# Moving the raw pair of heads to the front of a hand-ordered attention and expert kernel

## The chip, the cores and the metric

The kernel runs on one core of a Trainium2 chip. The metric is the time of one execution on the device in microseconds (us); of several runs the median is given. The core has engines that run side by side, each through its own instructions in order: TensorE (PE in the profile, with PEld for its weight loads), VectorE (DVE), ScalarE (ACT), GpSimd (POOL) and SyncE (SP). POOL, SP and ACT also start transfers (DMAs), which 16 DMA engines carry out.

## The reference

Sliding-window causal attention (8 batches, 8 heads, 576 positions, head size 64, window 64), then an expert layer: each batch picks one of 8 experts by its pooled attention output, and runs all its rows through that expert.

```python
scores = scale * np.matmul(q, k.transpose(0, 1, 3, 2))
mask = (rel >= 0) & (rel < window)
scores = np.where(mask, scores, -1000000000.0)
attn = np.exp(scores)
attn = attn / (np.sum(attn, axis=-1, keepdims=True) + 1e-09)
attn_out = np.matmul(attn, v)
...
x = np.ascontiguousarray(attn_out.transpose(0, 2, 1, 3)).reshape(B, S, H * D)
pooled = x.mean(axis=1)
logits = pooled @ w_gate
e_idx = np.argmax(logits, axis=1)
...
h = np.maximum(x[mask] @ w1[e], 0.0)
out[mask] = gate_w[mask, None, None] * (h @ w2[e])
```

## The kernel before, in words

The work of a batch is cut into five units: four pairs of heads over the first 512 positions, and a fifth "tail" unit for the last 64 positions of all heads. Units are numbered through the batches: 0 to 3 are the pairs of batch 0 and 4 its tail, 5 to 8 and 9 belong to batch 1, and so on to 39. Pair 1 holds heads 2 and 3.

The order of all instructions is written out by hand in the list `OPS` (lines 2 to 38), which has 890 entries. A loop at line 537 runs through it and issues for each entry the instructions of one step. Each step belongs to one engine, and each engine executes its own steps in the order of the list. An entry has a letter, perhaps a small letter for the engine or the buffer, and a number: of the unit, of the batch, or of a transfer.

Steps of a unit, in the order in which they depend on each other:

- `T` (line 214): on PE, transposes of the pair's queries and keys into PSUM, 16 matmuls (8 for a tail). With `m` the result goes to one of three shared PSUM buffers (`mo`, in turn), without it to a buffer of its own, of which there is one.
- `U` (line 238) copies the transposed queries to SBUF, `k` (line 249) the keys; `a` stands for ACT and `d` for DVE.
- `S` (line 257): scores on PE. With `b` the mask is first added by two matmuls with the identity (line 269), without it the later step `K` (line 295) multiplies by the mask on DVE. With `m` the scores take two of the three shared PSUM buffers, else they go to one buffer pair of their own.
- `E` (line 279): exponential on ACT. One instruction, or two where the scores lie in two shared buffers.
- `l` (line 303): row sums on PE. `n` and `R` (lines 347 and 354): logarithm and exponential of its negative on ACT, which give the reciprocal of the sum.
- `A` (line 318): attention times V on PE. `X` (line 360): on DVE, times the reciprocal, with a running sum for the gate.

Steps of a batch: `g`, `j`, `G`, `H`, `I` compute the gate (lines 378 to 439), `P` (line 411) reads the number of the expert into a register of POOL, `V` (line 148) shifts V in SBUF by two copies on DVE, for which four of the batch's five V transfers must have landed. Expert steps: `c` issues the next chunk of expert matmuls on PE (a batch has nine for the first weight and nine for the second, lines 450 and 494), `ra` and `rd` empty a chunk's PSUM buffer on ACT or DVE, `O` and `o` store a result.

Transfers: `Q` (line 104) loads queries (even number) or keys (odd) of a batch for all heads, or for some of them (`Q0.48`: queries of batch 0, heads 4 to 7; `Q1.2`: keys of batch 0, heads 0 and 1; `Q3`: all keys of batch 1). `L` (line 137) loads a fifth of a batch's V (`L4`, `L9` and so on are half as large), `t` (line 130) the tail rows of queries and keys, `W` (line 416) a quarter of the picked expert's weights: `W0` and `W1` of the first weight of batch 0, `W2` and `W3` of the second. All of these are issued by POOL, and POOL's transfers, which convert from float32, share one software queue. Only `Y` (line 116) differs: it brings queries (`Y0.24`) and keys (`Y1.24`) of heads 2 and 3 of batch 0 over SP's queue, raw in float32, and `Cd` (line 123) converts them on DVE. This is the pair that comes raw, unit 1.

Setup: `i` makes the identity and `y` the band of the mask on POOL (lines 176 and 180), `mb` and `Mb` build the masks on DVE (lines 186 and 199), `z` clears parts of the V buffers on DVE (line 195).

The loads of queries, keys and tails have three buffers each, and V has three, so a transfer for batch 3 waits until batch 0's data have been read.

Of the kernel before, what the change touches and what calls it, by code (L numbers as in the profile page):

```python
# [1 line left out]
OPS = (  # L2
    "Y0.24 Q0.48 Q1.48 Q0.2 Cd0.24 y i Q1.2 Y1.24 Q3 Cd1.24 z Tm3 Tm2 mb T0 Tm1 ka3 ka2 ka0 "
    "t0 Ud3 Ud2 Q2 Sb3 L0 L3 ka1 L1 L2 E3 Smb2 L4 Ud0 l3 Ud1 t1 S0 T4 E2 kd4 Ud4 n3 Smb1 E0 "  # L4
    "Mb K0 E1 R3 Q4 L9 Tm5 Sb4 Tm7 Tm8 Ud5 Q5 ka5 kd8 E4 L5 kd7 l1 n1 T6 l4 n4 Ud7 l2 Sb5 ka6 "
    "n2 R1 R4 l0 V0 A3 Ud6 L7 Am1 n0 E5 T9 X3 Am2 Ud9 S7 R2 L8 E7 Ud8 X1 R0 l5 X2 L6 n5 Smb6 "
    "A0 Am4 K7 ka9 E6 t2 X4 X0 Sb8 l7 g0 n7 T12 j0 Q6 Sm9 Tm10 G0 Ud12 kd12 E8 Ud10 H0 E9 "
    "Tm13 Tm11 R7 K9 l6 R5 ka10 Sb12 Ud11 ka13 V1 n6 Q7 l8 P0 Ud13 W0 I0 kd11 T14 Am5 A7 X7 "
    "A6 Ud14 kd14 L12 n8 X5 E12 R6 l12 n12 Sm14 X6 S11 l9 E14 Smb10 Tm17 E11 n9 T18 W1 Ud17 "  # L9
    "A9 W2 E10 S13 kd18 Ud18 L13 Tm15 Ud15 l10 Am8 R8 W3 kd15 ka17 T16 K14 L11 c X8 L14 n10 "  # L10
    "E13 R9 c ra X9 c R10 c rd c g1 K11 rd S17 j1 G1 ra ra c H1 L10 c rd l14 K13 c t3 ra c P1 "
    "n14 Q8 ra c c rd c V2 Ua16 c c ra ka16 l11 A10 X10 Am12 W4 c Q9 R12 X12 n11 ra W5 R11 "
    "A11 rd W6 T19 E17 c l13 n13 R13 Ua19 I1 X11 c Sm18 S15 K17 L15 rd E18 W7 R14 A13 c l17 "
    "ra X13 A14 c L16 L17 X14 g2 n17 Tm20 E15 ra kd19 c Ud20 ra L18 kd20 T22 S19 Sm16 E19 L19 "
    "j2 G2 c P2 t4 K15 E16 Q10 K18 c ra c W8 H2 ra ka22 c ra c c S20 l18 ra rd rd K16 c n18 "
    "Q11 K19 L21 ra Tm21 c c Ua21 Ud22 l16 W9 T23 R17 kd21 L23 V3 c c R18 c ra Am17 Ud23 n16 "
    "ra l15 E20 X17 L22 c R16 ka23 c rd n15 A18 c S23 X18 Sm21 K20 T24 kd24 ra R15 E21 L20 "
    "A16 c l19 L29 ra L24 W10 n19 Ud24 Am15 X16 A19 W11 R19 c X15 l20 E23 n20 L25 I2 c X19 rd "
    "L26 ra Tm26 c g3 K23 kd26 l23 Ud26 R20 c ra Sm22 n23 S24 j3 rd G3 E24 E22 T28 H3 K21 c "
    "Tm27 Ud28 P3 t5 ka27 kd28 l21 L28 rd n21 I3 K24 S26 L27 T25 c V4 W12 c Ua27 ra l24 c K22 "  # L20
    "c ra ra ra Ud25 n24 c R23 Q13 Q12 Am20 X20 R21 c c c rd Am23 W13 kd25 E26 A21 T29 rd X23 "
    "l22 Sm27 W14 W15 n22 E27 S28 V5 c c K26 K27 L32 c R24 l26 c X21 t6 A24 E28 Am22 ra R22 "
    "L30 ra K28 n26 X24 Ud29 kd29 c A27 l27 n27 c X22 ra ra c g4 S25 R26 rd Sm29 j4 G4 L34 "
    "E29 T32 Tm30 kd30 E25 Ud30 c Ua32 H4 K29 P4 ka32 ra c l28 R27 T33 L33 rd Ua33 S30 I4 n28 "
    "c Q15 c ra L31 ra Am26 ka33 c E30 c ra W16 X27 X26 ra l29 c K25 R28 c rd n29 Q14 A28 K30 "
    "c W17 X28 T34 S32 Sm33 ra O O E32 c E33 c K32 l25 n25 R25 c kd34 Am25 A29 W18 c O Ua34 "
    "R29 rd W19 T31 l30 c X29 X25 rd ka31 g5 c c Ud31 O ra K33 rd Sm31 n30 S34 j5 G5 c V6 R30 "
    "P5 rd O E31 H5 c K31 T36 l32 Ud36 rd E34 c t7 c A30 c n32 I5 rd L39 ka36 ra R32 l33 T35 "
    "X30 A32 Ua35 L38 rd c K34 rd c ka35 c n33 T37 ra Sm35 S36 L37 O E35 rd c X32 ra E36 W20 "
    "l34 c L35 n34 c K35 K36 L36 c kd37 R33 c O l31 rd W21 R34 rd c n31 R31 c Ua37 Tm38 O W23 "  # L30
    "Ud38 A33 ra ka38 Am34 l35 T39 X33 c n35 W22 c ra X34 A31 X31 g6 kd39 c O Sm38 R35 O S37 "
    "ra E38 j6 c c G6 P6 Ud39 E37 ra ra c V7 K38 rd H6 c l36 c K37 W24 n36 S39 A35 l37 ra rd "
    "E39 c ra n37 c X35 R36 c A37 c ra l38 Am36 K39 ra c c O R37 rd X37 n38 Am39 X36 O c rd c "
# [560 lines left out]
```

## Time and profile before

| what | us |
|---|---|
| median of 3 runs (lowest to highest) | 204.35 (203.72 to 204.58) |
| the profiled execution's own time | 203.52 |
| its span in the trace | 201.9 |
| PE busy in the span | 183.5 |
| ACT busy | 131.8 |
| DVE busy | 119.9 |
| POOL busy (mostly issuing transfers) | 111.0 |

The profiled execution took 203.52 us, 1.6 more than the span that the trace covers. All rows of the trace count from the start of the span. A busy share is an average over a span whose parts have different limits, so it is read by stretches. In rows of the timeline the columns are start, duration, engine, line, operation, output and input, and in square brackets how long the engine had been idle and what ended that. In rows of groups the columns are busy us, mean ns of one, and idle time ahead with its releasers.

### The profile page before, as it was taken

What the parts mean: (1) busy time and instruction counts of PE and PEld (TensorE: products, weight loads), DVE (VectorE), ACT (ScalarE), POOL (GpSimd) and SP (SyncE); (2) the same over time, 40 slices, a digit from 0 to 9 for tenths busy, and PEclk for the clock granted to TensorE, in tenths of its full rate; (3) what the DMA queues carried; (4) which work ended last, traced back from release to release, by engine and by line L of the source; (5) the groups of instructions that cost most, each with busy time, mean ns of one, the idle gap of its engine ahead of it and who ended that gap; (6) DMA issues with size and microseconds to landing.
All of it is one profiled execution on the core that took longest, in us unless ns stands there. A gap on an engine that the chain in (4) does not pass through costs nothing.

```text
span 201.9 us, 8105 instructions
## 1 busy us (share of the span) xinstructions
PE 183.5 (91%) x3518; PEld 124.2 (62%) x3522; DVE 119.9 (59%) x347; ACT 131.8 (65%) x247; POOL 111.0 (55%) x158
## 2 busy tenths in 40 slices
PE   0487886899999999999999999999999999999991
PEld 0455564656677756577667666676656666776760
DVE  3527989595477546895877457966494651216410
ACT  2179998876599578977779975757787436321121
POOL 7985939235931593478633552439452716553561
PEclk9999999999999999999999999999999999999998
DMA  6999999999999999999999999999999999999693
GB/s 135 175 188 159 194 162 198 199 198 174 196 201 197 170 198 193 174 201 167 200 206 200 169 195 223 259 208 137 183 237 243 266 254 212 274 212 301 235 325 134
DMA packets 83346, 41.16 MB, mean 204 GB/s; under 512 B 48080, under 2 KB 80976, under 8 KB 83312
## 3 DMA queue, kind: packets, MB, share of 16 engines
q0 software_dynamic: 81936, 39.72, 138.5%
q1 hardware_dynamic: 768, 0.85, 1.3%
q8 instruction: 27, 0.44, 0.8%
q10 hardware_dynamic: 608, 0.08, 0.2%
q14 instruction: 7, 0.06, 0.1%
HBM read 61.88 MB, written 9.44 MB: 353 GB/s over the span
## 4 chain that ended last, share of the span: by engine, by line
PE 77%; DMA 9%; POOL 7%; issue 3%; DVE 2%; ACT 1%; POOLq 0%; DVEq 0%; ACTq 0%
PE ph L461 28%; PE po L503 25%; DMA vw<-in_v_dram 9%; PE tp L225 5%; PE ph L470 4%; PE s L275 4%; PE av L331 3%; PE po L512 3%; PE lb L309 3%; POOL vw L141 2%; POOL km L110 2%; POOL qm L110 1%; POOL out_dram L492 1%; PE gps L392 1%; POOL qkt L133 1%
## 5 line engine op out<-in xcount | busy, mean ns | idle before, releaser
L503 PE MATMUL po<-w2b,hm 128*64 128x512 f16 x512 | 60.1, 379 | 0.0
L461 PE MATMUL ph<-xm,w1b 128*64 128x512 f16 x512 | 60.0, 379 | 0.0
L461 PEld LDWEIGHTS <-w1b 128*64 128x64 f16 x512 | 31.7, 110 | 18.7 <-issue 0.4
L503 PEld LDWEIGHTS <-hm 128*64 128x64 f16 x512 | 30.1, 110 | 19.3
L141 POOL DMA_DIRECT2D vw<-in_v_dram x32 | 28.9, 910 | 13.3 <-DMA w1b<-in_moe_w_dram 4.3
L446 ACT ACTIVATE hm<-ph,gw 128x512 f16<-128x512 f32 x39 | 26.6, 693 | 13.4 <-PE ph L461 13.3
L492 POOL DMA_DIRECT2D out_dram<-ob x31 | 17.2, 557 | 25.0 <-DMA w1b<-in_moe_w_dram 7.0
L351 ACT ACTIVATE ln<-lb 128x512 f32<-128x512 f32 (+1 forms) x40 | 22.5, 563 | 11.8 <-PE lb L309 8.6
L364 DVE CUSTOM_DVE_ANT_0 xm<-av,rl 128x512 f16<-128x512 f32 x32 | 21.6, 686 | 10.4 <-PE av L331 9.5
L482 ACT COPY ob<-po 128x512 f32<-128x512 f32 x18 | 10.6, 586 | 23.6 <-PE po L503 23.6
L448 DVE TENSOR_SCALAR hm<-ph,gw 128x512 f16<-128x512 f32 x25 | 18.7, 748 | 12.1 <-PE ph L461 11.6
L357 ACT ACTIVATE rl<-ln 128x512 f32<-128x512 f32 (+1 forms) x40 | 23.3, 594 | 1.5 <-DVE pool L364 1.3
L225 PE MATMUL tp<-ident,qm 128*64 128x128 bf16 x256 | 13.8, 232 | 7.4 <-DMA qm<-in_q_dram 6.9
L288 ACT ACTIVATE pe<-s 128x1024 f16<-128x1024 f32 x19 | 19.5, 1028 | 1.4 <-PE s L275 0.7
L297 DVE TENSOR_TENSOR pe<-pe,mask 128x1024 f16<-128x1024 f16 x24 | 16.3, 687 | 3.9 <-ACT pe L288 3.1
L252 ACT COPY kT<-tp 128x512 bf16<-128x512 bf16 x19 | 11.2, 597 | 9.0 <-PE tp L225 8.0
L225 PEld LDWEIGHTS <-qm 128*64 128x64 bf16 x256 | 10.7, 118 | 10.0 <-DMA qm<-in_q_dram 6.9
L482 DVE COPY ob<-po 128x512 f32<-128x512 f32 x14 | 9.7, 690 | 10.7 <-PE po L503 10.5
L423 POOL DMA_DIRECT2D w1b<-in_moe_w_dram x16 | 12.6, 785 | 5.9 <-DMA vw<-in_v_dram 2.9
L275 PEld LDWEIGHTS <-kT 64*128 64x128 bf16 x576 | 10.1, 95 | 8.9 <-issue 5.6
L331 PEld LDWEIGHTS <-vw 128*64 128x64 f16 x512 | 12.4, 112 | 4.7 <-issue 1.2
L225 PE MATMUL tp<-ident,km 128*64 128x128 bf16 x256 | 13.9, 231 | 1.4 <-DMA km<-in_k_dram 0.9
(80 smaller groups left out, 267.2 us busy)
## 6 DMA issues: line engine op xcount, KB each, us to landing
w1b<-in_moe_w_dram POOLq DMA_DIRECT2D x16, 512.0 KB, 9.3
w2b<-in_moe_w_dram POOLq DMA_DIRECT2D x16, 512.0 KB, 13.4
out_dram<-ob POOLq DMA_DIRECT2D x31, 256.0 KB, 8.1
vw<-in_v_dram POOLq DMA_DIRECT2D x32, 128.0 KB, 9.0
km<-in_k_dram POOLq DMA_DIRECT2D x7, 512.0 KB, 9.3
qm<-in_q_dram POOLq DMA_DIRECT2D x7, 512.0 KB, 9.0
out_dram<-obt POOLq DMA_DIRECT2D x14, 64.0 KB, 7.7
qkt<-in_q_dram POOLq DMA_DIRECT2D x8, 64.0 KB, 7.6
```

Of the source, the lines that this page charges most:

```text
L141: nc.gpsimd.dma_start(out=vt[:, 2 * J + 1], in_=v[b, :, 128 * J:128 * J + 128].rearrange("h c d -> c h d"))
L225: nc.tensor.transpose(tp[p0:p0 + 64, n, r], t[:, 2 * i + hh, ts(r, 64)], ident)
L288: nc.scalar.activation(out=po, in_=sp[0], func=AF.Exp, scale=scale)
L351: nc.scalar.activation(out=ln, in_=lb[:, 0:n], func=AF.Ln)
L357: nc.scalar.activation(out=rl, in_=lns.pop((b, i)), func=AF.Exp, scale=-1.0)
L364: nc.vector.tensor_tensor_reduce(out=xm[:, i], in0=av.rearrange("q r p -> q (r p)"), in1=rl, scale=1.0, scalar=0.0, op0=ALU.mult, op1=ALU.add,
L446: nc.scalar.activation(out=o, in_=i, func=AF.Relu, scale=g)
L448: nc.vector.tensor_scalar(out=o, in0=i, scalar1=g, scalar2=0.0, op0=ALU.mult, op1=ALU.max)
L461: nc.tensor.matmul(out=ph[64 * c:64 * c + 64], lhsT=w1t[:, kb, ts(2 * ft + c, 64)], rhs=xm[:, kb], start=(kb == 0), stop=(kb == 3), skip_g ...
L482: copy(e)(out=ob, in_=po)
L492: (nc.scalar if n and eng is nc.sync else eng).dma_start(out=dst, in_=src)
L503: nc.tensor.matmul(out=po[64 * c:64 * c + 64], lhsT=hm[:, fb, ts(2 * r + c, 64)], rhs=w2t[:, fb], start=(fb == 0), stop=(fb == 7), skip_gr ...
```

## The change

The list `OPS` alone changes. Its first 262 entries are put in another order; the remaining 628 are the same. The number of units, chunks and transfers is the same, and so is the number of scores steps with `b` in the changed part (nine). Some steps change their engine or their buffer: in the changed part the k copies of units 0, 1, 3, 10 and 17 go from ACT to DVE and those of 7, 14 and 18 from DVE to ACT; the q copies of units 4, 7, 13 and 18 go from DVE to ACT and that of 16 from ACT to DVE; the scores of units 0, 7 and 14 gain `b`, those of 2, 5 and 8 lose it (and get a step `K` instead); several steps gain or lose `m`.

The raw pair's transposes, `T1`, stand first on PE, followed by `Tm3`, `Sb1`, `Tm2`, `T4`, `Smb3`, `Tm0`. On POOL the identity `i` moves ahead of the second load, the tails `t0` and the keys `Q3` of batch 1 ahead of the loads `Q0.2` and `Q1.2` of heads 0 and 1; later `L4` comes ahead of `L2`, `Q5` ahead of `Q4`, `t2` ahead of `L7`, `W1` to `W3` ahead of the V of batch 2, `Q8` ahead of `P1` and `t3`, and `L15` ahead of `W5`. The list up to where the two orders meet:

```diff
-    "Y0.24 Q0.48 Q1.48 Q0.2 Cd0.24 y i Q1.2 Y1.24 Q3 Cd1.24 z Tm3 Tm2 mb T0 Tm1 ka3 ka2 ka0 "
-    "t0 Ud3 Ud2 Q2 Sb3 L0 L3 ka1 L1 L2 E3 Smb2 L4 Ud0 l3 Ud1 t1 S0 T4 E2 kd4 Ud4 n3 Smb1 E0 "
-    "Mb K0 E1 R3 Q4 L9 Tm5 Sb4 Tm7 Tm8 Ud5 Q5 ka5 kd8 E4 L5 kd7 l1 n1 T6 l4 n4 Ud7 l2 Sb5 ka6 "
-    "n2 R1 R4 l0 V0 A3 Ud6 L7 Am1 n0 E5 T9 X3 Am2 Ud9 S7 R2 L8 E7 Ud8 X1 R0 l5 X2 L6 n5 Smb6 "
-    "A0 Am4 K7 ka9 E6 t2 X4 X0 Sb8 l7 g0 n7 T12 j0 Q6 Sm9 Tm10 G0 Ud12 kd12 E8 Ud10 H0 E9 "
-    "Tm13 Tm11 R7 K9 l6 R5 ka10 Sb12 Ud11 ka13 V1 n6 Q7 l8 P0 Ud13 W0 I0 kd11 T14 Am5 A7 X7 "
-    "A6 Ud14 kd14 L12 n8 X5 E12 R6 l12 n12 Sm14 X6 S11 l9 E14 Smb10 Tm17 E11 n9 T18 W1 Ud17 "
-    "A9 W2 E10 S13 kd18 Ud18 L13 Tm15 Ud15 l10 Am8 R8 W3 kd15 ka17 T16 K14 L11 c X8 L14 n10 "
-    "E13 R9 c ra X9 c R10 c rd c g1 K11 rd S17 j1 G1 ra ra c H1 L10 c rd l14 K13 c t3 ra c P1 "
-    "n14 Q8 ra c c rd c V2 Ua16 c c ra ka16 l11 A10 X10 Am12 W4 c Q9 R12 X12 n11 ra W5 R11 "
-    "A11 rd W6 T19 E17 c l13 n13 R13 Ua19 I1 X11 c Sm18 S15 K17 L15 rd E18 W7 R14 A13 c l17 "
+    "Y0.24 Q0.48 Y1.24 i Q1.48 y z Cd0.24 t0 Cd1.24 mb T1 Ud1 Tm3 Q3 kd1 Sb1 Tm2 Ud3 Q0.2 E1 "
+    "Q1.2 kd3 ka2 Ud2 T4 Smb3 L3 E3 Tm0 kd4 S2 Ud0 l1 Q2 kd0 E2 n1 Ua4 L0 Smb0 E0 Tm7 Ua7 T5 "
+    "R1 Tm8 L1 l3 Mb Sb4 Ud8 ka7 E4 n3 Ud5 Tm6 l4 L4 ka5 ka6 K2 Sb7 L2 n4 l2 kd8 t1 T9 V0 R3 "
+    "n2 Ud6 ka9 Sm5 A1 X1 R4 E5 Am3 X3 R2 Q5 Am2 K5 X2 l0 Smb6 A0 Ud9 L9 Q4 n0 l5 E7 n5 R0 "
+    "Am4 S9 t2 l7 E9 S8 n7 X4 L7 X0 L8 T12 E6 L5 g0 K9 j0 L6 Ud12 Tm10 Tm11 E8 G0 kd12 H0 T14 "
+    "Q6 R5 kd10 Ud14 l9 Ud11 Tm13 Ud10 kd11 I0 Sb12 Q7 n9 R7 l6 ka13 P0 W0 ka14 Smb14 V1 n6 "
+    "Ua13 W1 R9 Am5 W2 W3 E14 K8 Am6 E12 A7 X5 l8 R6 Smb10 L12 X7 X6 S11 n8 E11 l12 n12 T17 "
+    "kd17 S13 E10 A9 Tm18 X9 L11 ka18 Ud17 Tm15 Ua18 A8 K11 l10 L14 R8 kd15 Ud15 L10 T16 ka16 "
+    "c X8 E13 c L13 c n10 rd ra c ra g1 S17 j1 G1 R10 c rd c K13 c rd R12 ra c c H1 l14 rd c "
+    "ra Q8 n14 P1 c c l13 ra V2 c t3 Ud16 n13 W4 c ra A12 Q9 X12 E17 L15 l11 ra Am10 n11 c I1 "
+    "X10 R11 A11 W5 T19 rd c c K17 R13 X11 Sm18 Ua19 W6 S15 rd E18 W7 R14 A13 c l17 ra X13 "
...
```

34 rows, old and new, of the table OPS are left out of this document.

## The prediction

> **What bounds the kernel now.** I first read the stretches: the span cut where the chain of waits changes hands (columns: stretch, its length, then busy us and instruction count of PE, PEld, DVE, ACT, POOL, then clock, DMA share, GB/s).
>
> ```profile
> core 0 of [0], span 201.9 us
> ...
> 0.00:6.88 6.88, 0.00 (x2) 0.01 (x2) 3.33 (x14) 1.28 (x1) 5.49 (x13) 1.00 0.82 145
> 6.88:12.50 5.62, 4.37 (x65) 3.48 (x66) 1.68 (x5) 2.34 (x4) 5.32 (x7) 1.00 1.53 179
> 12.50:20.34 7.84, 6.54 (x158) 4.37 (x158) 3.99 (x10) 6.99 (x13) 5.01 (x7) 1.00 2.04 172
> 20.34:31.32 10.98, 8.87 (x235) 6.08 (x236) 9.53 (x34) 10.71 (x23) 7.65 (x10) 1.00 1.87 180
> 31.32:36.16 4.84, 2.88 (x102) 2.39 (x102) 4.78 (x12) 3.89 (x8) 4.48 (x6) 1.00 1.42 200
> 36.16:40.84 4.68, 4.18 (x126) 3.23 (x127) 2.31 (x7) 4.06 (x9) 1.45 (x2) 1.00 1.46 198
> ...
> 53.98:197.60 143.62, 143.53 (x2646) 97.12 (x2642) 86.04 (x242) 94.16 (x177) 73.29 (x106) 1.00 1.37 216
> ```
>
> From 53.98 on PE idles 0.09 us in 143.62: there the kernel is bound by PE, and that part of the list is unchanged. All idle time of PE that can be won lies ahead of the first expert chunk: 6.88 + 1.25 + 1.30 + 2.11 + 1.96 + 0.50 = 14.0 us. From 20.34 to 31.32 ACT is busy 10.71 of 10.98. Next I read the chain that ended last.
>
> ```profile
> 22.68 8.52 DMA vw<-in_v_dram
> ...
> 40.09 0.22 PE lb L309 x2
> 40.31 0.25 PE av L331 x16
> 40.56 0.45 PE tp L225 x16
> ...
> 45.33 0.34 PE s L275 x16
> ```
>
> Columns: start, length, what. It goes through a transfer of V, then stays on PE almost to the end. So PE is held at the start by loads, then by ACT and DVE, and the first chunk ("c1") is the point after which nothing is held. The change can move the end only by moving c1. The PE rows also give my prices on PE: row sums (l) 0.22, AV (A) 0.25, transposes of a pair (T) 0.45, scores (S) 0.34.
>
> Last the timeline, at the places that the order is about.
>
> ```profile
> 4.79 0.43 DVE L128 CAST km<-raw 128x512 bf16<-128x512 f32 x1 [0.35 <-DMA raw<-in_k_dram]
> ...
> 6.88 0.64 PE L225 MATMUL tp<-ident,qm 128*64 128x128 bf16 x8 [6.88 <-DMA qm<-in_q_dram]
> ...
> 8.83 0.64 PE L225 MATMUL tp<-ident,qm 128*64 128x128 bf16 x8
> ...
> 9.26 0.64 PE L225 MATMUL tp<-ident,km 128*64 128x128 bf16 x8
> ...
> 12.97 1.02 ACT L288 ACTIVATE pe<-s 128x1024 f16<-128x1024 f32 x1 [0.73 <-PE s L275]
> ```
>
> The raw pair is cast by 4.79 + 0.43 = 5.22, but PE stands at 6.88 for heads 6 and 7, and the first exponential runs at 12.97. Early transposes come 9.26 - 8.83 = 0.43 per eight, 0.86 a pair: half the later pace.
>
> **The change part by part.**
>
> *The loads are one line of transfers.* The tile view, over windows that hold one or two issues, gives times from issue to landing:
>
> ```profile
> L110 POOL DMA_DIRECT2D km<-in_k_dram x1: 790/790/790, 2.3 to 2.3; - x1
> DMA to landing us min/median/max: 6.0/6.0/6.0
> ```
>
> ```profile
> L110 POOL DMA_DIRECT2D km<-in_k_dram x2: 730/821/912, 4.8 to 5.5; - x2
> DMA to landing us min/median/max: 4.9/5.9/6.8
> ```
>
> ```profile
> L133 POOL DMA_DIRECT2D qkt<-in_k_dram x1: 688/688/688, 7.1 to 7.1; - x1
> DMA to landing us min/median/max: 6.1/6.3/6.5
> ```
>
> ```profile
> L110 POOL DMA_DIRECT2D km<-in_k_dram x1: 878/878/878, 27.8 to 27.8; - x1
> DMA to landing us min/median/max: 9.0/9.0/9.0
> ```
>
> ```profile
> L423 POOL DMA_DIRECT2D w1b<-in_moe_w_dram x1: 752/752/752, 30.0 to 30.0; - x1
> DMA to landing us min/median/max: 9.4/9.4/9.4
> ```
>
> Landings: Q1.48 at 2.3 + 6.0 = 8.3, Q1.2 at 9.7, Q3 at 5.5 + 6.8 = 12.3, the tails t0 at 7.1 + 6.1 = 13.2, Q7 at 36.8, W0 at 39.4. Q3 follows Q1.2 by 2.6 us and W0 follows Q7 by 2.6 us, both 512 KB: the transfers land in the order of their issue at about 200 GB/s. So a landing is set by what stands ahead of it on POOL's queue. Ahead of W0 stands the same set in both lists, so W0 stays at 39.4 whatever the engines do.
>
> *The head.* SP's two raw loads stay the first two of its queue. On POOL, `i` moves ahead of Q1.48 and `y` behind it (0.3 us later for Q1.48, hidden since the line is full), t0 ahead of Q3, and Q0.2 and Q1.2 behind both. `z` moves into DVE's wait for the raw rows: nothing. T1 then runs from about 4.5 to 5.9 instead of last. But T3 stands between it and Sb1, and its keys still land at 8.3 and take 0.43. Sb1 has no row at the slow pace: E1 starts between 8.75 + 0.34 = 9.1 and some 10.4 (an estimate: its 18 products at twice S's and T's later times), 2.6 us or more ahead of 12.97. I take 10.4; the next wait hides the difference.
>
> *The added wait.* Q1.2 now lands at 8.3 + 0.9 (t0) + 2.6 (Q3) + 0.65 + 0.65 (the halves of two heads, 2.6 / 4 each) = 13.1. PE stands at Tm0 until then. Queued behind it are S2, l1, Smb0, T7, T5, T8; Ud0 and kd0 on DVE and E2 and E0 on ACT wait for those. T 0.45, S 0.34: E2 starts about 14.0; an exponential takes 1.0 (the row at 12.97), n1 and Ua4 stand between, so E0 ends near 16.7. Before, four exponentials and n3 followed 12.97: near 17.4. The lead of 2.6 us has become 0.7.
>
> *Copies.*
>
> ```profile
> L252 ACT COPY kT<-tp 128x512 bf16<-128x512 bf16 x19 | 11.2, 597 | 9.0 <-PE tp L225 8.0 <-DVE qt L242 0.9
> ...
> L242 DVE COPY qt<-tp 128x512 bf16<-128x512 bf16 x25 | 10.4, 417 | 8.0 <-PE tp L225 3.6 <-ACT kT L252 3.2 <-PE s L275 1.2
> ...
> L252 DVE COPY kT<-tp 128x512 bf16<-128x512 bf16 x13 | 8.8, 684 | 2.8 <-PE tp L225 1.9 <-ACT qt L242 0.9
> ```
>
> ```profile
> 20.34 0.89 DVE L150 COPY vw<-vw 64x2048 f16<-64x2048 f16 x1 [0.54 <-DMA vw<-in_v_dram]
> ...
> 25.12 0.62 ACT L357 ACTIVATE rl<-ln 128x512 f32<-128x512 f32 x1
> ...
> 28.73 0.13 DVE L407 TENSOR_SCALAR gnm<-gmx 128x1 f32<-128x1 f32 x1
> ...
> 31.32 0.87 DVE L150 COPY vw<-vw 64x2048 f16<-64x2048 f16 x1
> ```
>
> Three k copies leave ACT's first stretch (3 x 0.60 = 1.8 us; 0.68 each on DVE, which waits at Tm0 anyway), but ka7, ka9, Ua4, Ua7 and n5 come ahead of R0, some 2.4 us with the tails (4, 9) at half price. So R0 starts near 25.12 + 0.6 = 25.7. V0 needs L2, which now has half a V transfer (L4, some 0.45) more ahead of it: 20.8 instead of 20.34, and A1, X1 and all behind them with it. V0 to gate is the same work on DVE less Ud8 (0.42), plus K9: the gate stays near 28.7, W0's issue near 30. DVE then has kd12, kd10, kd11, Ud11, Ud10 and the tail Ud14 ahead of V1, 3 x 0.68 + 2.5 x 0.42 = 3.1 us: V1 starts near 32.0 instead of 31.32, though its V rows land at 22.7 + 8.5 = 31.2 plus the 0.5 of t2, which moves ahead of L7. Up to here nothing is won.
>
> *The last stage before c1.* Here the gain arises.
>
> ```profile
> 38.68 0.38 PE L225 MATMUL tp<-ident,km 128*64 128x128 bf16 x7 [0.50 <-issue]
> ...
> 40.84 0.38 PE L461 MATMUL ph<-xm,w1b 128*64 128x512 f16 x2
> ```
>
> Before, PE is busy 4.18 of the 4.68 us up to c1 (the row 36.16:40.84): it is late with work, not with data, W0 having landed 1.4 us earlier. In the new order T14 and Smb14 come ahead of V1, and S10 ahead of T17. After Q7 lands at 36.8 PE has left: half of T17 0.22, S13 0.34, A9 0.13, T18 and T15 0.90, A8 0.25, l10 0.22, T16 0.45, together 2.5 us: 39.3. ACT's line: from R0 at 25.7 to the end of E10, which l10 needs, are 25 instructions; at the 10.98 / 23 = 0.48 us of the stretch in which it was full that is 37.7, and l10 comes at 38.7, so 1.0 us of waiting is covered. So PE is free for c1 at 39.3, and W0 lands at 39.4. I add 0.3 us for hand-overs between engines that such a sum leaves out (bounds: 0, and 0.73, V1's lateness in full) and take c1 = 39.75, a gain of 40.84 - 39.75 = **1.1 us**. The floor of W0 caps it at 1.4.
>
> *After c1* the steps up to A12 hold 14 chunks, as did those up to A10, and V2 caps the gain once more:
>
> ```profile
> 51.76 0.76 DVE L151 COPY vw<-vw 64x2048 f16<-64x2048 f16 x1
> ```
>
> ```profile
> 53.98 0.67 PE L331 MATMUL av<-pe,vw 128*64 128x64 f16 x32
> ```
>
> V2 ends at 52.5, and A10 began at 53.98: the same set of transfers stands ahead, so at most 1.4 can be kept; 1.1 passes. W1 to W3 move ahead of batch 2's V, L15 ahead of W5 and Q8 ahead of P1 and t3; I cost these at nothing. Their cover is PE's unbroken work from 53.98 on; without it W5, one V transfer of 0.9 us later, could hold PE by up to that. The list's last 628 entries are unchanged and carry the shift to the end.
>
> Sum against the profiled execution: 203.52 - 1.1 = 202.4; against the median 204.35, which is 0.8 above it: **203.2 us**.
>
> *A rule that speaks against it.* PE's transposes came 0.43 per eight at 8.83 and 0.45 per sixteen at 40.56. The Trainium skill, "TensorE: Matmul & The Clock Gate", section "Part 1: The HAM clock gate", says that an idle PE runs at half clock until a window of about 3.4 us was busy, and falls back after an idle one; the two rows agree, and the page would make nothing of the order itself but of its gaps. What follows from rows alone is rival C.
>
> **The rivals.** A: *DVE eats the gain.* V1 starts 0.7 us later than before, and PE's idle 0.50 at 38.68, whose cause the trace doesn't show, comes again. For: both lie on the path. Against: S14 and T14 are done by then. c1 = 39.35 + 0.73 + 0.50 = 40.6, a gain of 0.2: 204.1.
>
> B: *Slower, through Tm0.* If Q1.2 takes as long from its issue (about 7.1) as Q7 took, 9.0, instead of the 6.0 that my line of transfers comes to, it lands at 16.1, 3.0 later, and PE, ACT and DVE all stand. ACT, nearly full until 31.32, hands this on whole. From 1.1 us of lateness on the kernel is slower than before; at 3.0 c1 = 39.75 + 3.0 = 42.75, 1.9 worse: 206.3. For: nothing in the old order put whole loads ahead of these halves. Against: the line adds up so evenly.
>
> C: *PE stays slow.* Before, the slow pace lasted from 6.88 to about 12.5. The new order has gaps at 6 to 8.4 and at 13, so if the pace changes only after T0, T7, T5 and T8 cost 0.43 more each, 1.3 us, of which the wait for V0 hides some 0.5: c1 at 40.55, 204.1.
>
> **How the numbers follow.** Forecast 0.52, A 0.22, C 0.08, B 0.18. Forecast's own range: gain 0.7 to 1.4, 202.95 to 203.65, widened by the spread of a median. A measurement tells about 0.5%, 1.0 us, from no change. Of the forecast 0.42 lies beyond it. Faster 0.42; same 0.10 + 0.22 + 0.08 = 0.40; slower 0.18. The range reaches from the cap of 1.4 with half a us for the median's spread to a B of 1.9 us, and leaves out what lies beyond: 202.5 to 205.1.
>
> **What would show it.** Right: T1 before 5; PE idle at Tm0 until about 13; V0 near 20.8; V1 near 32; W0's landing at 39.4 and c1 within 0.5 behind it; later stages shifted alike. Wrong: W0 landing elsewhere (then the line of transfers is not a line), E10 after 39 (A), Tm0 after 14.5 (B), pairs still spaced 0.43 per eight after 14 (C), or PE idle between c1 and 60.

## The result and the profile after

The new order is slower: 205.28 us in the median of 22 runs (203.92 to 206.86) against 203.88 of 22 runs before (203.15 to 205.05), ratio 1.0069, 95% interval 1.0049 to 1.0089. I had forecast 203.2, with 0.18 on slower. The profiled execution took 206.8 us (span 205.2, before 203.52 and 201.9), so it lies at the long end of the new order's runs; the sums below are made against that execution, and the spread is taken up in the experiments. Ratios, here and below, leave out the few runs that lie over 1.5% above the fastest of their kernel.

First the stretches of the new kernel, cut where those of before were cut (stretch, its length, busy us and count of PE, PEld, DVE, ACT, POOL, then clock, DMA share, GB/s).

```profile
0.00:6.88 6.88, 1.91 (x24) 1.19 (x24) 4.01 (x18) 1.28 (x1) 5.46 (x13) 1.00 0.86 151
6.88:12.50 5.62, 4.50 (x54) 2.40 (x56) 2.22 (x5) 1.58 (x2) 5.17 (x7) 1.00 1.43 155
12.50:20.34 7.84, 3.89 (x93) 2.65 (x94) 1.45 (x4) 3.98 (x8) 3.83 (x5) 0.97 1.86 159
20.34:31.32 10.98, 9.15 (x208) 6.27 (x205) 7.84 (x24) 9.57 (x20) 7.64 (x9) 0.87 1.90 176
...
53.98:201.00 147.02, 146.81 (x2678) 98.83 (x2674) 87.54 (x245) 94.94 (x180) 76.17 (x110) 1.00 1.38 213
```

PE starts earlier, as it was meant to (1.91 us busy by 6.88, before 0.00). The head start is gone by 20.34: between 12.50 and 20.34 PE works 3.89 us instead of 6.54, DVE 1.45 instead of 3.99, ACT 3.98 instead of 6.99. All three stand, so they stand for something that none of them makes. The transfers too run at 155 and 159 GB/s where they ran at 179 and 172. The clock column shows 0.97, and in the next stretch 0.87. From 53.98 on PE is as full as before, so the loss must lie ahead of the first expert chunk (c1). PE's timeline at the place:

```profile
4.50 0.32 PE L225 MATMUL tp<-ident,qm 128*64 128x128 bf16 x2 [4.50 <-DVE qm L128]
...
13.24 0.41 PE L225 MATMUL tp<-ident,qm 128*64 128x128 bf16 x8 [0.16 <-DMA qm<-in_q_dram]
13.92 0.41 PE L225 MATMUL tp<-ident,km 128*64 128x128 bf16 x8 [0.27 <-DMA km<-in_k_dram]
...
15.48 0.41 PE L275 MATMUL s<-qt,kT 64*128 64x64 bf16 x16
19.42 0.41 PE L225 MATMUL tp<-ident,qm 128*64 128x128 bf16 x8 [3.52 <-DMA qm<-in_q_dram]
19.66 0.51 PE L225 MATMUL tp<-ident,km 128*64 128x128 bf16 x8
19.96 0.64 PE L225 MATMUL tp<-ident,qm 128*64 128x128 bf16 x8
20.38 0.64 PE L225 MATMUL tp<-ident,km 128*64 128x128 bf16 x8
...
43.76 3.41 PE L461 MATMUL ph<-xm,w1b 128*64 128x512 f16 x30
```

The wait that I had added up, at Tm0, is there and is short (13.24 and 13.92). The one that costs stands four steps later, at Tm7: 3.52 us until Q2, the queries of batch 1, has landed. Behind it the transposes come 0.42 us apart per eight, half the later pace. The clock column agrees: cut finely it stands at 0.50 from 19.79 to 23.21 and at 1.00 on both sides. One stretch of it:

```profile
20.00:21.00 1.00, 1.00 (x24) 1.00 (x22) 0.00 (x0) 0.79 (x2) 0.91 (x2) 0.50 2.07 171
```

(It doesn't tell of every slow stretch: before 12.5 it shows 1.00, though eight transposes take 0.43 us there too.) c1 is at 43.76 (before 40.84), 2.92 us late, and the span is 3.3 us longer. What hangs on DVE, and W0 on POOL:

```profile
23.90 1.05 DVE L150 COPY vw<-vw 64x2048 f16<-64x2048 f16 x1
...
33.38 0.13 DVE L407 TENSOR_SCALAR gnm<-gmx 128x1 f32<-128x1 f32 x1
36.37 0.69 DVE L150 COPY vw<-vw 64x2048 f16<-64x2048 f16 x1
```

```profile
34.69 1.50 POOL L423 DMA_DIRECT2D w1b<-in_moe_w_dram  x2 [4.40 <-DVE kT L252]
```

V0 comes 3.56 us later than before (20.34), the gate 4.65 (28.73), V1 5.05 (31.32), and POOL stands 4.40 us ahead of W0, whose address needs the gate; W0 lands at 41.2, not at 39.4. (Of these 1.8 us, 1.6 are those of Q7, the load ahead of it, which was issued at 29.4 for 27.8 and landed at 38.4 for 36.8.) From V1 to c1 the new order then needs 7.39 us where the old one needed 9.52: so the last stage does give back 2.1 us, as foreseen, but of a loss of 5. And the late transfer itself, in the view of its tile over a window with this one issue:

```profile
L110 POOL DMA_DIRECT2D qm<-in_q_dram x1: 903/903/903, 8.7 to 8.7; - x1
DMA to landing us min/median/max: 10.7/10.7/10.7
```

Issued at 8.7, landed at 19.4. Before, the same transfer left at 7.8 and took 8.0.

### The profile page after: what moved, and what is told of

Same layout as the page of the kernel before. It is cut to its first block, busy times and chain, and to the rows that moved or that the text cites. A ratio compares the mean times of both kernels' runs of the same rounds, so it can differ in the third digit from the quotient of the medians.

```text
span 205.2 us, 8106 instructions
## 1 busy us (share of the span) xinstructions
PE 187.0 (91%) x3522; PEld 125.9 (61%) x3522; DVE 121.1 (59%) x346; ACT 131.1 (64%) x248; POOL 111.6 (54%) x158
## 4 chain that ended last, share of the span: by engine, by line
DMA 36%; PE 35%; POOL 9%; issue 9%; ACT 7%; DVE 2%; POOLq 1%; ACTq 0%
DMA w2b<-in_moe_w_dram 20%; PE ph L461 11%; PE po L503 10%; DMA w1b<-in_moe_w_dram 8%; DMA qm<-in_q_dram 5%; PE tp L225 4%; DMA vw<-in_v_dram 3%; POOL out_dram L492 3%; PE s L275 2%; PE av L331 2%; ACT rl L357 2%; PE lb L309 2%; ACT ln L351 2%; POOL km L110 2%; POOL vw L141 2%
## 5 line engine op out<-in xcount | busy, mean ns | idle before, releaser
L446 ACT ACTIVATE hm<-ph,gw 128x512 f16<-128x512 f32 x38 | 25.8, 698 | 13.8 <-PE ph L461 13.5
L448 DVE TENSOR_SCALAR hm<-ph,gw 128x512 f16<-128x512 f32 x26 | 19.4, 748 | 11.9 <-PE ph L461 11.4
L288 ACT ACTIVATE pe<-s 128x1024 f16<-128x1024 f32 x18 | 18.6, 1033 | 9.3 <-PE s L275 8.0
L297 DVE TENSOR_TENSOR pe<-pe,mask 128x1024 f16<-128x1024 f16 x25 | 17.0, 686 | 3.5 <-ACT pe L288 2.8
L242 DVE COPY qt<-tp 128x512 bf16<-128x512 bf16 x23 | 9.4, 416 | 13.0 <-PE tp L225 10.9
L275 PEld LDWEIGHTS <-kT 64*128 64x128 bf16 x576 | 10.8, 97 | 10.2 <-issue 7.2
L291 ACT ACTIVATE pe<-s 128x512 f16<-128x512 f32 x28 | 15.2, 602 | 2.7 <-PE s L275 2.7
L426 POOL DMA_DIRECT2D w2b<-in_moe_w_dram x16 | 12.7, 802 | 5.6 <-PE ph L461 2.4
L423 POOL DMA_DIRECT2D w1b<-in_moe_w_dram x16 | 12.5, 782 | 5.8 <-DVE kT L252 4.4
```

The source lines that it names most:

```text
L288: nc.scalar.activation(out=po, in_=sp[0], func=AF.Exp, scale=scale)
L446: nc.scalar.activation(out=o, in_=i, func=AF.Relu, scale=g)
L448: nc.vector.tensor_scalar(out=o, in0=i, scalar1=g, scalar2=0.0, op0=ALU.mult, op1=ALU.max)
```

## The experiments

My theory (theory 1 in the first texts, "feed" in the later ones): the new order of the engines is fed by the loads in the wrong order, and the wait at Tm7 with what hangs on it is the loss. The rivals: the new order of the engines costs by itself; the late part of the list costs; and, beside the wait, the half pace of PE behind it. In the edits, entries of the list that stay are left out; a first chunk is the first row of line 461. All ratios are to the kernel before, run between the others on the same chip.

**The new order again** (no edit).

> The new order unchanged, for the spread and for a second trace. Theory 1 (PE stands at Tm7 for Q2, the queries of batch 1, which the new order of the loads brings late): PE is idle ahead of Tm7 for 1.5 to 4 us in this trace too, Q2 lands between 17 and 19.5, and the ratio to the kernel before is 1.003 to 1.010. Theory 2 (the order on PE, ACT and DVE itself is slower): the time is as slow, but also in a trace whose gap at Tm7 is short. Theory 3 (the slow pace of PE after the gap): the pairs after the gap are spaced 0.43 us per eight transposes.

Measured: 205.37 us (12 runs, 203.74 to 207.00), ratio 1.0060, interval 1.0034 to 1.0086. The loss is real, and so is the wait. The profiled execution, the longest of the twelve, has Q2 at 18.8, and PE's timeline there is:

```profile
18.81 0.64 PE L225 MATMUL tp<-ident,qm 128*64 128x128 bf16 x8 [2.52 <-DMA qm<-in_q_dram]
19.24 0.64 PE L225 MATMUL tp<-ident,km 128*64 128x128 bf16 x8
```

c1 is at 43.57. Here the half pace holds from the first transpose behind the wait on, since the clock fell to 0.50 at 17.87, during the wait, and stayed there until 24.70. The spread is wide too: the 22 runs above span 2.9 us where the 22 of the kernel before span 1.9.

**Which half of the change costs: the engines or the loads?** Two kernels, each with one half.

```diff
# e1_old_loads and e1_again: engines new, order of the transfers old
- Q0.48 i Q1.48 y t0 Q3 Q0.2 Q1.2 L3 Q2 L0 L1 L4 L2 ...
+ Q0.48 Q1.48 Q0.2 y i Q1.2 Q3 t0 Q2 L0 L3 L1 L2 L4 ...
# e2_new_loads: engines old, order of the transfers new (the same two lines, exchanged)
```

> The new order of steps on PE, ACT and DVE, with the loads and POOL's two setup steps in the old order. Theory 1: Q2 lands near 15.8 as before, PE's gap at Tm7 falls under 0.7 us, the first chunk starts between 39.4 and 40.3 and the ratio to the kernel before is 0.993 to 0.998 (202.5 to 203.5 us). Theory 2: the ratio stays at 1.004 to 1.010, as for the new kernel. Theory 3 says as theory 1 here, since without the gap the pace stays up.

> The old order of steps on PE, ACT and DVE, with POOL's loads and setup steps in the new order. Theory 1: the old order needs Q2 at Tm5, at 15.9, and it lands at 17 to 19.4; T0 needs Q1.2, which lands at 13.8, and stands first in the old order, so this is slower than the new kernel: ratio 1.010 to 1.025 (206 to 209 us). Theory 2: the loads cost little, ratio 0.998 to 1.004.

> The new engine order with the old order of loads once more, unchanged, since its profiled execution held an idle time of 2.08 us at 28.46 that no other run shows and that is put down to issue. If that idle time belongs to this order, it is there again and the first expert chunk stands at 43.5 to 44.5, median 205.2. If it came by chance, the profile shows the first chunk near 41 (T4's wait of 2.0 us alone, with V0 at 20.8), and the median comes out at 204.3 to 204.8.

Measured: e2 208.79 us, ratio 1.0264 (1.0233 to 1.0296). e1 205.22, 1.0069 (1.0044 to 1.0095), and again 204.85, 1.0053 (1.0024 to 1.0082). The new loads do hurt the old engines, far more than the new: T0, which the old order does early, stands 4.35 us for the queries of heads 0 and 1, until 13.99. But the old loads do not heal the new engines, which my theory had expected. PE's timeline of e1_again says why:

```profile
13.21 0.64 PE L232 MATMUL tpt<-ident,qkt 128*64 128x128 bf16 x8 [1.83 <-DMA qkt<-in_k_dram]
```

The new order does T4, the transposes of the tail, ahead of Smb3 and Tm0, and in the old order of loads t0 comes behind Q3 and lands at 13.0. Tm7 no longer waits; T4 does, and holds all that Tm7 held. The wait was exchanged, not removed. (The profile of the first of the two also stood 2.08 us at 28.46 with "issue" as releaser, its clock was 0.50 from 28.85 to 35.68, and its first chunk stood at 44.17; the repeat had neither, and its first chunk at 41.97. So this doesn't belong to the order.)

**Q2 alone, in the new order and in the old.**

```diff
# e3_q2_ahead (new order)
- Q0.2 Q1.2 L3 Q2 L0
+ Q0.2 Q1.2 Q2 L3 L0
# e6_old_q2late (old order)
- t0 Q2 L0 L3 L1 L2
+ t0 L0 L3 L1 Q2 L2
```

> The new kernel with one load moved: Q2 ahead of L3 on POOL. Theory 1: Q2 lands 1.5 to 2.5 us earlier, near 17, V0 stays within 0.5 us, since L3 is needed only for it; the first chunk comes 1 to 2 us earlier and the ratio to the kernel before is 0.996 to 1.002. If the lateness of the whole line of transfers counts more than this one place in it, Q2 lands after 18 and the ratio stays above 1.004.

> The old order with Q2 alone moved behind three V transfers (L0, L3, L1), as late as in the new order within some 1 us. Theory 'feed': Tm5, which starts at 15.94 before, waits until Q2 lands at about 18.5, 2.6 us; E4, E5 and what hangs on them come later by 1.5 to 2.6, the gate at 30 to 31, the time 204.8 to 206. Rival (the old order has room for a late Q2, the loss of the new order is elsewhere): within 0.5 us of before, 203.4 to 204.3.

Measured: e3 204.67 us, ratio 1.0043 (1.0014 to 1.0072); e6 207.84, ratio 1.0194 (1.0140 to 1.0248), more than I expected of it. PE's timelines, first of e3, then of e6:

```profile
17.52 0.41 PE L225 MATMUL tp<-ident,qm 128*64 128x128 bf16 x8 [0.95 <-DMA qm<-in_q_dram]
17.77 0.39 PE L225 MATMUL tp<-ident,km 128*64 128x128 bf16 x8
17.99 0.39 PE L225 MATMUL tp<-ident,qm 128*64 128x128 bf16 x8
...
40.47 3.62 PE L461 MATMUL ph<-xm,w1b 128*64 128x512 f16 x32
```

```profile
19.00 0.41 PE L225 MATMUL tp<-ident,qm 128*64 128x128 bf16 x8 [2.92 <-DMA qm<-in_q_dram]
...
20.37 0.64 PE L225 MATMUL tp<-ident,qm 128*64 128x128 bf16 x8
20.79 0.64 PE L225 MATMUL tp<-ident,km 128*64 128x128 bf16 x8
...
```

In e3, with one V transfer less ahead of Q2, Tm7 comes at 17.52 instead of 19.42, the pace behind it stays whole (0.22 per eight), and c1 stands at 40.47. Not all of these 1.9 us are the edit's: with the new order of loads unchanged Q2 lands at 17.8 (e10), 18.1 (e2), 18.8, 19.0 (e4) and 19.4 in the five traces; in e3 at 17.4. In e6 nothing but Q2 is moved, and the old order too stands 2.92 us and falls to half pace (clock 0.50 from 19.68 to 23.09); its c1 (44.91) comes 4.1 us later than before. So the place of Q2 is enough to make such a loss in either order.

**The pace behind the wait.** PE is given products of a constant to do while it stands at Tm7; no other work is changed. (They come in three entries `F`, one for each of the three shared PSUM buffers, so that the steps behind them keep their buffers.)

```diff
# e4_fill: 16 products; e10_fill_short: 9
- Smb0 E0 Tm7
+ Smb0 E0 F14 F1 F1 Tm7
+ Smb0 E0 F7 F1 F1 Tm7
```

> The new order with sixteen more 128x512 products of a constant in PE's queue ahead of Tm7, some 3.5 us at full pace, so that PE is busy while it waits for Q2; the loads are as in the new order. Theory 'wait' (the 3.5 us at Tm7 alone are the loss, handed on through ACT and DVE): the transposes behind Tm7 still start at 19.4 to 19.8, V0 stays within 0.3 of 23.6, the time stays at 205.3 (205.0 to 205.6). Theory 'wait and pace' (the idle PE falls back to half pace, 0.43 per eight transposes, and that adds to the wait in those executions in which it happens): transposes behind Tm7 come at 0.22 per eight, V0 and the first expert chunk 1 to 1.5 us earlier than in the new order, the time 204.0 to 204.6, and the spread over the runs shrinks from 3 us to about 1.5.

> The new order with nine products of a constant ahead of Tm7, some 2.0 us at full pace, so that they end near 18.3, ahead of Q2's landing (18.8 to 19.4 in the profiles), where the sixteen of the earlier run ended at 19.9 and held Tm7 back. Theory 'wait and pace': no half pace behind Tm7, the slow end of the spread (206 to 207) goes, the median comes to 204.6 to 205.0. Theory 'wait' alone: 205.2 to 205.5 and the same spread as the new order.

Measured: e4 206.88 us (206.18 to 208.51), ratio 1.0147 (1.0103 to 1.0192): a miss. The timeline shows the cause, the products end behind the load (Q2 had landed at 18.98):

```profile
16.31 3.63 PE L549 MATMUL wps<-warm 128*128 128x512 bf16 x16
19.87 0.41 PE L225 MATMUL tp<-ident,qm 128*64 128x128 bf16 x8
20.12 0.39 PE L225 MATMUL tp<-ident,km 128*64 128x128 bf16 x8
```

e10, whose products end at 18.1, 0.3 us behind the landing of Q2 in this execution (17.8):

```profile
16.07 2.12 PE L549 MATMUL wps<-warm 128*128 128x512 bf16 x8
18.12 0.41 PE L225 MATMUL tp<-ident,qm 128*64 128x128 bf16 x8
18.37 0.39 PE L225 MATMUL tp<-ident,km 128*64 128x128 bf16 x8
18.59 0.39 PE L225 MATMUL tp<-ident,qm 128*64 128x128 bf16 x8
```

204.73 us, within the 204.6 to 205.0 that I had given for the half pace as a part of the loss, and the runs lie between 204.20 and 205.81, where the 22 of the new order lie between 203.92 and 206.86. The ratio, 1.0060 (1.0039 to 1.0080), can't be told from that of the new order.

The granted clock, whose mean is known for every run, tells more of the median. The profiled executions that hold a stretch at 0.50 have a mean of 0.978 to 0.990, the others 0.994 to 1.000. Of the 22 runs of the new order twelve are at 0.990 or less, with a median of 205.98 us, and ten at 0.995 or more, with 204.94. Of the twelve runs of after_again five are at 0.990 or less; of the twelve of e10, where PE has work during the wait, two (205.79 and 205.81); of the 104 of the kernel before that ran beside the experiments, three. So about half of the new order's executions hold the half clock and take 1.0 us more (in after_again 1.6), and the others are slower than before too, by 1.1 us (in after_again by 0.3: 204.02 of seven runs against 203.77). This sorts runs by what befell them and is no experiment; e10 is one and points the same way, but its interval is too wide to show it for the median.

The runs now give the price of a late Tm7. In this table the start of Tm7, of c1, and the time between are read from the timelines shown or from the same view of the run (for before, Tm5, which waits for Q2 there):

| run | Tm7 | c1 | c1 - Tm7 | pace behind |
|---|---|---|---|---|
| before | 15.94 | 40.84 | 24.90 | whole |
| e3_q2_ahead | 17.52 | 40.47 | 22.95 | whole |
| e10_fill_short | 18.12 | 41.00 | 22.88 | whole |
| e5_fed | 18.18 | 41.28 | 23.10 | whole |
| e4_fill | 19.87 | 42.74 | 22.87 | whole |
| new order | 19.42 | 43.76 | 24.34 | half, 3.4 us long |
| after_again | 18.81 | 43.57 | 24.76 | half, 6.8 us long |

With the loads from t1 on in the new order and at whole pace, the new engines need 22.9 to 23.1 us from Tm7 to c1, for Tm7 anywhere from 17.5 to 19.9: each us of Tm7 is one us of c1. They are 1.8 to 2.0 us quicker than the old ones over this way. The half pace adds 1.2 to 1.5 us in the first trace that has it, and 1.7 to 1.9 in the second. (e1_again, with the old loads and T4's wait, needs 23.99.)

**Loads in the order of their use.**

```diff
# e5_fed (new engines)
- Q0.48 i Q1.48 y t0 Q3 Q0.2 Q1.2 L3 Q2 L0 L1 L4 L2
+ Q0.48 i Q1.48 y Q0.2 t0 Q1.2 Q3 Q2 L3 L0 L1 L2 L4
# e9_old_t0early (old order)
- Q1.2 Q3 t0 Q2
+ Q1.2 t0 Q3 Q2
```

> The new order of the engines, with the loads in the order in which that order uses them: Q0.48, i, Q1.48, y, Q0.2, t0, Q1.2, Q3, Q2, L3, L0, L1, L2, L4, then as in the new order. Theory 'feed' (the new engine order is good and only fed wrongly): t0 lands by 10, Q1.2 by 10.5, Q2 by 16, no PE wait of over 0.5 us at T4, Tm0 and Tm7, V0 at 20.8, first expert chunk at 39.6 to 40.2, the time 203.0 to 203.6, 0.2 to 0.8 under before. Theory 'engines' (the new order of DVE, ACT and PE costs by itself, whatever the loads): no waits there either, but the first chunk at 41 or later and 204.2 or more.

> The kernel before with t0 alone moved, ahead of Q3 instead of behind it. Theory 'thin line' (small transfers issued ahead of the whole ones leave the line of transfers without work, since a whole load lands no earlier than some 6.8 to 7.5 us behind its own issue and issuing the small ones takes 1.5 us): Q3 lands at 13.9 to 14.6, Q2 at 16.6 to 17.8, Tm5 waits for it, some 1 to 1.5 us, the time 204.6 to 205.5. Theory 'same line' (a landing is set by the bytes ahead of it alone, as the prediction had it): Q3 at 13.2, Q2 at 15.8, the time within 0.4 us of before.

Measured: e5 205.02 us, ratio 1.0038 (1.0012 to 1.0063). T4 and Tm0 no longer wait, but Tm7 does, 2.40 us, for Q2 lands at 18.1, not by 16. By the bytes ahead of it Q2 should have come as early as before. e9 shows what my line of transfers lacked. It moves t0 alone, ahead of Q3, and costs 1.9 us: 205.60, ratio 1.0113 (1.0067 to 1.0158). Tm5, which waits for Q2 in the old order, stands 2.48 us:

```profile
18.42 0.41 PE L225 MATMUL tp<-ident,qm 128*64 128x128 bf16 x8 [2.48 <-DMA qm<-in_q_dram]
```

The stretches of one us, first of before, then of e9:

```profile
9.00:10.00 1.00, 1.00 (x24) 1.00 (x22) 0.30 (x1) 0.65 (x2) 1.00 (x2) 1.00 1.38 181
10.00:11.00 1.00, 1.00 (x25) 1.00 (x22) 0.55 (x2) 0.73 (x2) 1.00 (x2) 1.00 1.45 197
11.00:12.00 1.00, 1.00 (x13) 0.49 (x10) 0.42 (x1) 0.73 (x2) 1.00 (x2) 1.00 1.85 173
```

```profile
9.00:10.00 1.00, 1.00 (x24) 1.00 (x22) 0.42 (x1) 0.73 (x2) 1.00 (x2) 1.00 1.50 72
10.00:11.00 1.00, 1.00 (x22) 0.87 (x18) 0.50 (x2) 0.62 (x2) 1.00 (x2) 1.00 0.95 95
11.00:12.00 1.00, 0.66 (x5) 0.13 (x2) 0.35 (x1) 0.59 (x1) 1.00 (x2) 1.00 1.19 153
```

POOL is busy for the whole of each (1.00), and the transfers fall to 72 and 95 GB/s, with the DMA share at 0.95 from 10 to 11 where it was 1.45: the line runs dry while POOL is still issuing. The tiles' view of e9, first Q3, then Q2:

```profile
L110 POOL DMA_DIRECT2D km<-in_k_dram x1: 895/895/895, 6.9 to 6.9; - x1
DMA to landing us min/median/max: 7.7/7.7/7.7
```

```profile
L110 POOL DMA_DIRECT2D qm<-in_q_dram x1: 898/898/898, 7.8 to 7.8; - x1
DMA to landing us min/median/max: 10.6/10.6/10.6
```

Q3, the next whole load, leaves 1.4 us later than before, because POOL issues t0's two transfers first, and lands 2.3 us later (14.6 instead of 12.3); Q2, which leaves as before, lands at 18.4 instead of 15.8. The new order of loads has t0 ahead of Q3 as well, and there the line ran at 133 and 131 GB/s from 7 to 9. One part isn't settled: with t0 early Q2 also follows the transfer ahead of it more slowly in some executions, by 2.6 to 3.8 us over the traces, with t0 late by 2.6 to 3.1.

**The new engines without any of these waits.** In steps, each from the one before: old loads with T4 behind l1; then the part from Q5 to L6 in the new order, since t2 came too late for T14; beside them the loads from Q6 on in the new order.

```diff
# e7_t4late = e1_old_loads and
- T4 Smb3 E3 Tm0 kd4 S2 Ud0 l1 kd0
+ Smb3 E3 Tm0 S2 Ud0 l1 T4 kd0 kd4
# e11_t2early = e7_t4late and
- t1 Q4 L9 Q5 L5 L7 L8 L6 t2 Q6
+ t1 Q5 L9 Q4 t2 L7 L8 L5 L6 Q6
# e8_t4late_newW, e12_t2early_newW = e7, e11 and
- W0 L12 W1 W2 L13 W3 L11 L14 L10 t3 P1 Q8
+ W0 W1 W2 W3 L12 L11 L14 L10 L13 Q8 P1 t3
# and, further on, L15 ahead of W5
```

> The new engine order with the old order of loads, and T4 with its copy kd4 moved behind l1, so that PE doesn't stand at T4 until t0 lands at 13.0 to 13.3. Theory 'feed' (the new engine order gains as soon as none of its steps waits for a load): Tm0 by 12, T4 at 13.0 to 13.4, Tm7 when Q2 lands, 15.7 to 16.1, the first expert chunk at 39.4 to 40.0 (W0 lands at 39.5), about 1 us ahead of before, the time 202.7 to 203.4. Theory 'engines' (the new order costs by itself): Tm7 as early as that, but the first chunk at 41 or later and the time at 204.2 or more.

> The kernel of the run before with the loads from Q6 on in the new order: W1, W2 and W3 ahead of L12, L11, L14, L10 and L13. Theory 'late loads cost' (in the traces so far the part from the first chunk to the end took 161.0 us with the old order of loads and 161.4 to 162.3 with the new one): the first chunk as in the run before, the time 0.4 to 1.2 us longer, 203.3 to 204.4, and PE idle at a weight matrix near 151. Theory 'nothing' (my prediction's value for that part): the same time within 0.3 us.

> As the run with T4 late, and besides Q5, L9, Q4, t2 ahead of L7, L8, L5, L6 as in the new order, since T14 stood 2.2 us until t2 landed at 31.8 there. All else of the loads is in the old order. Theory 'feed': Tm7 at 15.9 to 16.2, no wait of over 0.5 us at T14, V1 near 32.2, the first expert chunk at 39.4 to 40.2, the time 202.8 to 203.6, under before. Theory 'engines': the first chunk at 41 or later, 204.2 or more.

> The kernel of the run before with the loads from Q6 on in the new order (W1, W2, W3 ahead of L12, L11, L14, L10, L13). Theory 'late loads cost': the same first chunk, 0.4 to 1.2 us more from there to the end, the time 203.4 to 204.6. Theory 'nothing': within 0.3 us of the run before.

Measured: e7 204.56 us, ratio 1.0030 (1.0002 to 1.0059); e8 205.54, 1.0064 (1.0035 to 1.0093); e11 203.55, 1.0006 (0.9976 to 1.0037); e12 203.63, 0.9999 (0.9975 to 1.0023). PE's timeline of e7, then of e11:

```profile
15.99 0.41 PE L225 MATMUL tp<-ident,qm 128*64 128x128 bf16 x8 [0.53 <-DMA qm<-in_q_dram]
...
31.81 0.38 PE L232 MATMUL tpt<-ident,qkt 128*64 128x128 bf16 x7 [2.16 <-DMA qkt<-in_k_dram]
```

```profile
16.13 0.41 PE L225 MATMUL tp<-ident,qm 128*64 128x128 bf16 x8 [0.69 <-DMA qm<-in_q_dram]
...
30.17 0.41 PE L232 MATMUL tpt<-ident,qkt 128*64 128x128 bf16 x8 [0.49 <-DVE kT L252]
...
40.00 2.33 PE L461 MATMUL ph<-xm,w1b 128*64 128x512 f16 x20
```

e7 has Tm7 at 15.99, where I wanted it, and meets the next mismatch: T14, which the new order puts ahead of V1, waits 2.16 us for t2 (c1 at 41.76). e11 takes that away too, and c1 is at 40.00, 0.84 us ahead of before and within 0.3 of my forecast of 39.75. So with T4 moved the loss of the new order is a matter of feeding it, and its engines do not cost by themselves; the half clock is rare, too (one of the twelve runs has a mean of 0.990 or less). But the time is that of before, not less. With Tm7 this early the price of one for one has ended, too: from Tm7 to c1 e11 needs 23.87 us, 0.8 to 1.0 more than the table's, for V0 now waits 0.46 us for its rows (0.2 of it shows behind), a row sum at 25.41 comes some 0.4 later, and some 0.3 are lost near 37; what causes the last two isn't shown. W0 lands at 39.4 as forecast, 0.6 ahead of c1. e12 equals e11 within intervals of some 0.6 us: W1 to W3 ahead of the V loads cost nothing that these runs show. (e8 against e7 had suggested 1 us; their intervals overlap, and the first chunk of e8's profile was already late, at 42.71: behind T14's wait of 2.01 us its clock is 0.50 from 32.17 to 39.00.)

**Where e11's 0.84 us go.** From c1 to PE's last group (line 512) before needs 196.54 - 40.84 = 155.70 us, e11 196.77 - 40.00 = 156.77. Laid side by side group by group, e11's profile loses 0.55 of it between 89 and 98, where PEld stands for "issue", and 0.24 at 151.4, where W21's matrix is used:

```profile
PEld L503 <- issue: 0.5, 1, 0.5
```

```profile
151.17 0.39 PE L309 MATMUL lb<-pe,ones 128*64 128x512 f16 x2
151.62 1.05 PE L461 MATMUL ph<-xm,w1b 128*64 128x512 f16 x8
```

Before, the same two groups stand at 151.19 and 151.41, and W21 had landed at 150.5; in e11 it lands at 151.6, as the matrix is wanted. A last kernel moves W21:

```diff
# e13_w21early = e11_t2early and
- W20 L35 L36 O W21
+ W20 W21 L35 L36 O
```

> The first kernel of this call with one more move in the part that the change leaves alone: W21 ahead of L35, L36 and a store. In three runs whose first chunk was early or whose loads were late, PE stood at W21's matrix near 152 (0.17 to 0.48 us shown, 0.4 to 0.8 in all), and before it lands 0.9 us ahead of its use. Theory 'second floor' (a gain of over some 0.9 us ahead of the first chunk is lost again at W21): 0.3 to 0.8 us faster than the first kernel of this call, 202.3 to 203.0. Theory 'no floor there': the same time within 0.3.

Measured: 204.40 us (203.74 to 204.91), ratio 1.0031 (1.0009 to 1.0054): no gain, a miss. In its profile the part behind c1 does take 155.77 us, 1.0 less than in e11, and W21 lands at 147.6, 3.9 us ahead of its use; but c1 is at 41.00, though the list is the same up to there (ACT's exponentials release a row sum 0.79 us late at 25.87, where e11 has 0.28). So c1 differs by an us between executions of one list (40.00 and 41.00, both at full clock). In e12, whose list differs only behind W0, it is at 41.56, and there the clock is 0.50 from 28.35 to 31.76, with no wait of PE over 0.74 us in the five us ahead of it. Whether a second limit lies at W21 is therefore open; no version here beats the kernel before.

## Why the prediction was wrong, point by point

- *What bounds the kernel, and that c1 carries the end.* Right for a late c1: it came 2.92 us later and the span 3.3. From c1 to the end of the span the traces differ by 1.4 us (160.9 to 162.3), so a gain of 1.1 is not sure to arrive.
- *The head.* Right: T1 at 4.50 (said 4.5), the first exponential at 10.19 (10.4).
- *The loads are one line of transfers.* The order of landing was right, the rate wrong. I took 200 GB/s without a break. With t0 ahead of Q3 the line runs dry (72 and 95 GB/s in e9; 133 and 131 in the new order). The small transfers cost POOL's time to issue, not their bytes, and that delays the whole load behind them.
- *The added wait.* **This is the step that failed.** It counted S2, l1, Smb0, T7, T5 and T8 as queued behind Tm0, and asked for each what Tm0 gives it. It did not ask which load each needs of its own. T7 is the first to read Q2, and L3 had been put ahead of Q2. Its own rule would have shown it: Q1.2 at 13.1, L3 0.9 and Q2 2.6 give 16.6, just behind Smb0's end at 15.9 and so a wait of 0.7 us. It was 3.52 us, with Q2 at 19.4; the other 2.8 are the rate of the line, the term above, which was the larger error. The wait at Tm0 itself was in its place and 0.8 us under (13.92 for 13.1), and so was E0, whose row in ACT's timeline ends at 17.5 where I had 16.7. So the lead of 0.7 us that I had left was gone before Tm7, at the 17.4 of before:

```profile
16.37 1.12 ACT L291 ACTIVATE pe<-s 128x512 f16<-128x512 f32 x2
```

- *Copies.* The sums (V0 20.8, gate 28.7, V1 32.0) were undone by that wait: 23.90, 33.38, 36.37. In e11, where it is gone, they came out as 20.12, 29.29 and 32.27, and in e13 as 19.94, 29.75 and 32.73, so the step itself was sound to about 1 us.
- *W0 stays at 39.4 whatever the engines do.* Wrong: it landed at 41.2. That a landing follows the one ahead of it held: W0 came 2.8 us behind Q7, and 2.5 to 2.8 in all traces but two (e2 3.3, e1_old_loads 4.0). But Q7 itself was issued 1.6 us late, so late engines do reach the line, through the issue.
- *The last stage before c1.* Right in size: 7.4 us from V1 to c1 where I had 39.75 - 32.0 = 7.75, and c1 at 40.00 in e11.
- *After c1.* The late loads at nothing: not contradicted by e12. That the gain passes to the end: not shown; e11's 0.84 us were lost again, and e3, with c1 0.37 us ahead of before, has a span 0.4 us longer.
- *The rivals.* B had the direction and the price of a late load, at the wrong load: Q1.2 was not late, Q2 was. A didn't come. C, that PE stays slow, came in another form: in the new order's trace PE was at whole pace at 13.92, and fell back behind the wait; by the mean clocks this befell about half of the executions and cost those 1.0 to 1.6 us. (In e1_again eight transposes at 15.29 still took 0.42 us, C's own sign.) The Trainium skill, "TensorE: Matmul & The Clock Gate", section "Part 1: The HAM clock gate (the "warmup" mystery)", says that the window over which idleness counts is about 3.4 us and runs freely. The traces agree with the length: the clock stands at 0.50 for 3.4 us (new order, e6, e12) or for 6.8 us (after_again, e1_old_loads, e8). Which waits are followed by it they don't settle: those of 3.52, 2.92 (e6), 2.52 (after_again), 2.08 (e1_old_loads) and 2.01 us (e8) were, those of 2.40 (e5) and 2.48 us (e9) were not, and in e12 no wait over 0.74 us stood in the five us ahead of it.

## What to carry to other kernels

When a step is moved ahead, write down for each step behind it the load that it is the first to read, and when that load lands in the new order of issue: the wait that decides may stand some steps behind the one that was added. A queue of loads and an order of work are one schedule; moving either alone exchanged one wait for another here (Tm7, T4, T14), and only with all three repairs was the time that of before. A price per late us is worth measuring with a few places of one load: here it was one for one, over 22.9 us of work that looked loosely coupled. And when one kernel's executions differ by 3 us, sort them by the granted clock before you explain the median.

## What the runs showed of the hardware that was not expected

- Small transfers ahead of a whole one can starve the line: moving two transfers of 64 KB ahead of one of 512 KB in e9 made that land 2.3 us later. From issue to landing t0's halves took 3.9 to 6.9 us over the traces, Q2 and Q3 6.8 to 10.7. The Trainium skill, "DMA: Bandwidth & Descriptors", section "Anatomy of one DMA — SWDGE (gpsimd) path", gives a fixed 2.0 us plus the bytes at 436 GB/s for one transfer by GpSimd, an estimate of 2.2 and 3.2 us here. The shortest landings of t0 and Q3, 3.9 and 6.8, are about twice that; they have other transfers beside them, and no run shows one alone.
- The half pace of PE comes in stretches of one length. In the six traces that show it the granted clock is 0.50 for 3.41 us (19.79 to 23.21 in the new order; also e6 and e12) or for twice that (17.87 to 24.70 in after_again; also e1_old_loads and e8). PE need not be idle for as long ahead of it: in the 3.41 us before the clock fell PE was busy for 0.37 us (new order), 0.67 (e6), 1.33 (e8), 1.34 (e1_old_loads), 1.84 (e12) and 1.84 (after_again).
- Nor does it begin at a fixed place of the wait: the clock fell 0.4 us behind the end of the wait in the new order, 0.7 behind it in e6, and 0.9 ahead of it in after_again. So one list of instructions gives executions with and without it.
- PE stood for "issue", without a releaser that the profile shows, up to 2.08 us in one execution and not in the next of the same list.
